# One product for the Q table and one for the spectrum, by an eighth turn in both angle tables of an S4 convolution and bilinear GLU kernel

## The chip, the cores and the metric

The kernel runs on one core of one Trainium2 chip. The metric is device time in microseconds, the median of several executions. A profiled execution, of its own time, supplies the traces.

## The reference

One block with adaptive layer norm, in float32, for L = 2048 tokens of width D = 640: first an S4 convolution with N = 192 complex states a channel, then a bilinear GLU of width F = 1536.

```python
dt = jnp.exp(log_dt)[:, None]
logdA = dt * (A_re + 1j * A_im);  dB = dt * (B_re + 1j * B_im)
P = jnp.exp(logdA[:, :, None] * l[None, None, :])          # D x N x L
K = jnp.einsum("dn,dnl,dn->dl", Cc, P, dB).real            # the kernel, D x L
...                                                        # y = irfft(rfft(u) * rfft(K)) + u * Dskip
h = layernorm(x) * (1 + ca) + sa;  x = x + ga * S4(h)
h = layernorm(x) * (1 + cb) + sb;  x = x + gb * (((h @ w_gate) * (h @ w_up)) @ w_down)
```

The six modulation rows sa, ca, ga, sb, cb, gb come from silu(c) @ w_mod.

## The kernel before, in words

The work falls into two parts. The first, up to about 525 us, makes the convolution kernel K, its spectrum and the spectrum of the normed input, multiplies the two and transforms back. The second is the GLU in split float32r products, on PE almost alone.

**Kernel generation.** There are 40 blocks n (`NK`), each of 16 channels of D, and ten halves hf of four blocks each. A power exp(logdA l) is split into a product of two factors P and Q, one for the coarse and one for the fine part of l, each with a magnitude (`EP`, `EQ`) and an angle. Angles are 32-bit integers in which 2^32 is a whole turn, so that adding them wraps by itself. Tables grow on POOL:

- `tab_ph` (L680, once a half, for the first half in two pieces a = 0 and 1) writes the low angles `LH`: column 0 is a copy (L698), column 1 an add (L699), and `double` (L678) makes columns 2 to 7. One half of the rows of LH is for P, the other for Q with the phase of the amplitude in it. L697 completes the high angles `DH`.
- `tab_eq` (L702) does the same for the magnitudes `LQ` (L708, L709, L678).
- `mk_ph`, `mk_eq` and `mk_ep` (all at L714 in `outer`) spread low and high parts into the block's tables `Ph`, `EQ` and `EP`, on POOL, for the next block.

ACT then makes a sine and a cosine of each angle (`trig`, L753, ACT instructions at L230) into a pair of PSUM banks `tr`, bank 0 the cosine and bank 1 the sine. The absolute value first and a quarter turn in the second call make the cosine. DVE multiplies by the magnitudes: `PtA` and `PtB` (L776, L796) for P, and `qmul` (L767) for Q. `QtA` covers 16 rows and `QtB` 8. Each Q row has 64 places. The first 32 (L769) hold the products with the angles in reversed order. The other 32 hold cosine times magnitude (L770) and minus sine times magnitude (L771). PE multiplies P and Q over the states: `kg_ma` (L811) from the A tiles, `kg_mb` (L826) from the B tiles, 32 small matmuls each, with the cosine half (c = 0) and the sine half (c = 1) added in PSUM, which gives the real part.

**Transforms.** `u_k` (L848) and `u_pre` (L872) do the first stage for K and for the input, `u_g` and `u_c` the second (`stage2`, L893). `u_c` (L919) multiplies the two spectra: real and imaginary part of K's spectrum (`kr`, `ki`, in PSUM) by both parts of H, in four products (L934 to L937) and two sums (L939, L940); then PE transforms back (L950), and `u_d` (L971, L978) ends it. Of the 20 products, 16 take all 128 channels at once and the last four are cut into two of 64 channels.

**Order.** Every engine works through its own queue in the order in which the program issues, which is written out by hand: a loop of 3 x 40 + 24 slots takes kg_aq, kg_ap and kg_b of block n in turn, issues the products of DVE in `MUL`, then POOL's tables for block n + 1, then PE's products, and fits all other jobs in by due times from the table `SCHED`. The buffers that two stages share (`Ph`, `PtA`, `TV`, `tr`) are two deep, and `QtA`, `QtB` and `PtB` one deep.

Of the kernel before, what the change touches and what calls it, by code (L numbers as in the profile page):

```python
# [12 lines left out]
I32 = mybir.dt.int32  # L13
AF = mybir.ActivationFunctionType
OP = mybir.AluOpType
# [3 lines left out]
P = 128  # L19
# [76 lines left out]
    d=(  # L96
# [5 lines left out]
    ),  # L102
# [68 lines left out]
    tr="abababababababababababababababababababababababababababababababababababababababababababababababababababababababababababab"  # L171
# [53 lines left out]
def tile_kernel(ctx: ExitStack, tc: tile.TileContext, I, out):  # L225
    nc = tc.nc
    V, S, G, PE, SY = nc.vector, nc.scalar, nc.gpsimd, nc.tensor, nc.sync

    def act(o, i, f=AF.Copy, **kw):
        return S.activation(o, i, f, **kw)  # L230

    const = ctx.enter_context(tc.tile_pool(name="const", bufs=1))
# [14 lines left out]
    shl = const.tile([P, 11], I32, name="shl")  # L247
    for k in range(11):
        V.memset(shl[:, k : k + 1], k + 1)
    mv1 = const.tile([P, 16, 2], F32, name="mv1")  # L250
    rs1 = const.tile([P, 16], F32, name="rs1")
    nm1 = const.tile([P, 16], F32, name="nm1")
# [8 lines left out]
    def ring(pool, shape, name, dtype=F32):  # L261

        return pool.tile(shape, dtype, name=name + next(slot[name]), bufs=1)
# [3 lines left out]
    def mark(*k):  # L267
        done[k] = done.get(k, 0) + 1

    def need(n, *k):  # L270

        assert done.get(k, 0) >= n, k
# [401 lines left out]
    def double(lo, powers, op):  # L674

        for w, p_ in zip((2, 4), powers):
            b = p_.unsqueeze(len(p_.shape)).to_broadcast(list(p_.shape) + [w])
            G.tensor_tensor(lo[..., w : 2 * w], lo[..., 0:w], b, op=op)  # L678

    def tab_ph(hf, a=None):  # L680

        need(1, "step", hf)
        if a != 1:
            need(1, "seeds", hf // 2)
        if hf:
            need(1, "ph", 4 * hf - 1)
        if a != 1:
            mark("lh", hf)
        dl, dh = DL[hf % 2], DH[hf % 3]
        sel = (lambda t: t) if a is None else (lambda t: t.rearrange("p (s a r) -> p s a r", a=2, r=24)[:, :, a])  # L690
        lh = LH if a is None else LH.rearrange("p (s a r) l -> p s a r l", a=2, r=24)[:, :, a]
        d = [sel(dl[:, k]) for k in range(4)]
        one = lambda t: t.unsqueeze(len(t.shape))
        if a != 1:
            for f in PSI.pop(hf):
                f()
        G.tensor_tensor(sel(dh[:, 3]), sel(dh[:, 1]), sel(dh[:, 2]), op=OP.add)  # L697
        G.tensor_copy(lh[..., 0:1], one(d[0]))  # L698
        G.tensor_tensor(lh[..., 1:2], one(d[0]), one(d[1]), op=OP.add)  # L699
        double(lh, d[2:], OP.add)  # L700

    def tab_eq(hf):  # L702
# [64 lines left out]
    def qmul(Qt, tr, e, R):  # L767

        return [lambda: V.tensor_tensor(Qt[:, :, :, 0:32], tr[:, :, :, ::-1], e[:, :, 0:32].unsqueeze(1).to_broadcast([P, 2, R, 32]), op=OP.mult),  # L769
                lambda: V.tensor_tensor(Qt[:, 0, :, 32:64], tr[:, 0], e[:, :, 32:64], op=OP.mult),  # L770
                lambda: V.scalar_tensor_tensor(Qt[:, 1, :, 32:64], tr[:, 1], -1.0, e[:, :, 32:64], op0=OP.mult, op1=OP.mult)]  # L771

    def kg_ap(n):
        PtA = OUT[n]["PA"]
# [3 lines left out]
    def kg_aq(n):  # L778
        QtA = pk.tile([P, 2, 16, 64], F32, name="QtA", bufs=1)
        OUT[n] = dict(QA=QtA, PA=ring(pk, [P, 2, 16, 32], "PtA"))  # L780
        ab = None
        if n:
            ab = OUT[n]["PA"].rearrange("p c r m -> p c (r m)")
            act(ab, PH[n].rearrange("p (a r) m -> p a (r m)", a=2)[:, :, 0:512], AF.Abs, scale=TURN)
            ab = ab[:, 1]
        tr = trig(PH[n].rearrange("p r m -> p (r m)")[:, 768:1280], ab)
        MUL.append(qmul(QtA, tr.rearrange("p c (r m) -> p c r m", m=32), EQ[n % 2][:, 0:16], 16))

    def kg_b(n):
        PtB = pk.tile([P, 2, 8, 32], F32, name="PtB", bufs=1)  # L790
        QtB = pk.tile([P, 2, 8, 64], F32, name="QtB", bufs=1)
        OUT[n].update(PB=PtB, QB=QtB)
        ep_ = EP[n % 2]
        tr = trig(PH[n].rearrange("p (a r) m -> p a (r m)", a=2)[:, :, 512:768])
        trv = tr.rearrange("p c (a r m) -> p c a r m", a=2, m=32)
        MUL.append([lambda: V.tensor_tensor(PtB, trv[:, :, 0], ep_[:, 16:24, :].unsqueeze(1).to_broadcast([P, 2, 8, 32]), op=OP.mult)]  # L796
                   + qmul(QtB, trv[:, :, 1], EQ[n % 2][:, 16:24], 8))
# [88 lines left out]
    def stage2(src, k0, r):  # L886

        need(1, "tw")
        for i in range(4):
            for c in range(2):  # L890
                for par in range(2):
                    k = 2 * i + par
                    PE.matmul(r[c][par * 64 : par * 64 + 64, i, :], t_tw[:, k0 + k, c, :], src[:, k, :], start=True, stop=True, tile_position=(0, par * 64))  # L893
        return r

    def banks():
        return [ring(PF[-1], [P, 4, P], "psf") for _ in range(2)]
# [21 lines left out]
    def u_c(db, qd, parts=1):  # L919

        k0, dn = 8 * qd, P // parts
        for d0 in range(0, P, dn):
            need(dn // 16, "F", db, d0)
            if parts == 1:
                r = banks()
            else:
                ps = ring(PF[-1], [P, 2, 4, dn], "psf")
                r = [ps[:, 0], ps[:, 1]]
            kr, ki = stage2(FS[db][:, k0 : k0 + 8, d0 : d0 + dn], k0, r)
            yield  # L930
            need(1, "GH", db, qd)
            H = GH[db, qd][..., d0 : d0 + dn]
            T = ring(fp, [P, 2, 4, dn], "TV")
            V.tensor_tensor(T[:, 0], kr, H[:, 0], op=OP.mult)  # L934
            V.tensor_tensor(T[:, 1], kr, H[:, 1], op=OP.mult)
            V.tensor_tensor(kr, ki, H[:, 1], op=OP.mult)
            V.tensor_tensor(ki, ki, H[:, 0], op=OP.mult)  # L937
            x = T if parts == 1 else H
            V.tensor_tensor(x[:, 0], T[:, 0], kr, op=OP.subtract)  # L939
            V.tensor_tensor(x[:, 1], T[:, 1], ki, op=OP.add)  # L940
            yield
        if parts > 1:
            x = GH[db, qd]
        need(1, "ti")
        r = banks()
        for i in range(4):
            for c in range(2):
                for par in range(2):
                    lo = par * 64
                    PE.matmul(r[par][:, i], t_ti[lo : lo + 64, qd * 4 + i, c, :], x[lo : lo + 64, c, i, :], start=c == 0, stop=c == 1, tile_position=(lo, 0))  # L950
        yield
        W = ring(fp, [P, 4, 2, P], "W")
        for par in range(2):
            act(W[:, :, par], r[par])
        WQ[len(PF) - 1].dma_start(WD[db][:, k0 : k0 + 8], W.rearrange("p i r d -> p (i r) d"))
        mark("WD", db)
# [329 lines left out]
    for db in range(NB):  # L1286
        if db:
            at(T0["q"][db - 1], u_seeds, db)
        for q in range(4):
            at(T0["pre"][db][q], u_pre, db, q)  # L1290
            at(T0["g"][db][q], u_g, db, q)
            at(T0["c"][db][q], u_c, db, q, 1 if db < NB - 1 else 2)
            at(T0["d"][db][q], u_d, db, q)
    for n in range(NK):
        at(T0["k"][n], u_k, n)
    for i, f in enumerate((tab_ph, tab_eq)):
        for hf in range(1, 2 * NB):
            at(T0["low"][i][hf - 1 : hf], once(f), hf)
# [17 lines left out]
    for i, _ in enumerate(gp0):  # L1316
        due(i - 100)
        if i == P_PH:
            tab_ph(0, 1)
            mk_ph(0, 1)  # L1320
        elif i == P_EP:
            mk_ep(0)
        elif i == P_MOD:
            mod_i()
    tab_eq(0)
    tab_ph(0, 0)
    mk_ph(0, 0)
    mk_eq(0)
# [538 lines left out]
```

## Time and profile before

| | us |
|---|---|
| median of 3 runs | 987.37 |
| lowest and highest | 986.79, 993.78 |
| the profiled execution, own time | 988.54 |
| its span, first to last instruction | 986.8 |
| busy in the span: PE, DVE, ACT, POOL | 889.2, 723.8, 579.4, 509.1 |
| mean granted clock of PE | 0.961 of full |

A row of the timeline has start, duration, engine, line, operation, what it writes and reads, and the shape; brackets give how long the engine stood idle before it and what ended that. A row of the chain has start, length, engine and line. A row of the stretches has the busy time of each engine in it with the number of instructions, then the granted clock (1.00 is full), the DMA share and GB/s. A row of the waits has the waiting engine and line, what it waited for, the sum in us, how often, and the longest.

### The profile page before, as it was taken

How to read it: one execution, taken by the hardware profiler on the slowest of the kernel's cores; microseconds unless marked ns; L12 is line 12 of the kernel's file. 1: busy time of each engine (PE TensorE's matmuls, PEld its weight loads, DVE VectorE, ACT ScalarE, POOL GpSimd, SP SyncE). 2: the span in 40 equal slices, each digit the busy share in tenths (PEclk: the TensorE clock that was granted, in tenths of full speed). 3: DMA queues.
4: the chain of work that ended last, by engine and by line, in shares of the span. 5: the costliest groups of instructions: out<-in, count | busy, mean ns of one | idle time of the engine just before them, and what ended most of it. 6: DMA issues, size and time to landing. Idle time of an engine off the chain costs nothing.

```text
span 986.8 us, 26765 instructions
## 1 busy us (share of the span) xinstructions
PE 889.2 (90%) x11134; PEld 720.2 (73%) x11134; DVE 723.8 (73%) x1400; ACT 579.4 (59%) x1076; POOL 509.1 (52%) x400
## 2 busy tenths in 40 slices
PE   4867898799789789988879999999999999999998
PEld 3565556586476557667736888889999788888998
DVE  8789568888978888794857665457676756578952
ACT  4869989987888887863336333334355443435430
POOL 5978899699879979960030354440113122222110
PEclk9877979999989889999999999999999999999999
DMA  7746654556246534658595665733564676658875
GB/s 254 262 142 223 204 194 147 172 165 185 77 153 181 152 105 126 205 172 257 189 273 191 222 191 182 242 125 113 184 217 124 197 231 222 222 179 292 237 244 187
DMA packets 158817, 188.54 MB, mean 191 GB/s; under 512 B 9828, under 2 KB 128360, under 8 KB 157544
## 3 DMA queue, kind: packets, MB, share of 16 engines
q1 hardware_dynamic: 149480, 155.51, 49.4%
q0 software_dynamic: 4752, 21.63, 7.6%
q10 hardware_dynamic: 4464, 9.70, 2.6%
q8 instruction: 87, 1.43, 0.6%
q14 instruction: 34, 0.28, 0.1%
HBM read 124.22 MB, written 62.59 MB: 189 GB/s over the span
## 4 chain that ended last, share of the span: by engine, by line
PE 55%; DVE 14%; ACT 12%; issue 10%; POOL 4%; DMA 3%; SPq 0%; DVEq 0%; POOLq 0%; ACTq 0%
PE pa L1078 18%; PE psg L1078 9%; PE pa L1502 9%; PE psfc L893 2%; PE kg L826 2%; PE kg L811 2%; PE psfa L893 2%; PE psfb L893 2%; ACT trb L230 1%; ACT tra L230 1%; PE psfc L950 1%; POOL EQ L714 1%; PE psfb L950 1%; PE pa L1554 1%; ACT L230 1%
## 5 line engine op out<-in xcount | busy, mean ns | idle before, releaser
L1055 POOL TENSOR_TENSOR tf<-wur,wgb 128x256 f32<-128x256 f32 x23 | 17.8, 775 | 246.9 <-DVE wtl L1026 199.5
L714 POOL TENSOR_TENSOR EQ<-LQ,RH 128x1536 f32<-128x1536 f32 x40 | 124.1, 3104 | 9.7 <-DVE QtB L771 9.5
L1026 DVE TENSOR_TENSOR wtl<-tf,wth 128x256 fp32r<-128x256 f32 (+1 forms) x72 | 36.7, 513 | 59.7 <-ACT wth L230 59.7
L714 POOL TENSOR_TENSOR Phb<-LH,DH 128x1536 int32<-128x1536 int32 x20 | 62.2, 3112 | 13.9 <-ACT tra L230 13.9
L714 POOL TENSOR_TENSOR EP<-LP,RH 128x768 f32<-128x768 f32 x40 | 66.0, 1650 | 0.0
L714 POOL TENSOR_TENSOR Pha<-LH,DH 128x1536 int32<-128x1536 int32 (+1 forms) x21 | 62.4, 2971 | 2.3 <-ACT trb L230 2.0
L1502 PE MATMUL pa<-wsg,sh 128*128 128x384 f32 (+1 forms) x304 | 58.4, 311 | 0.0
L826 PE MATMUL kg<-QtB,PtB 64*32 64x64 f32 x2560 | 48.7, 229 | 5.8 <-DVE QtB L770 5.3
L826 PEld LDWEIGHTS kg<-QtB,PtB 64*32 64x32 f32 x2560 | 41.7, 114 | 16.1 <-issue 7.2
L1502 PEld LDWEIGHTS pa<-wsg,sh 128*128 128x128 f32 x304 | 45.7, 189 | 0.0
L1541 POOL DMA_DIRECT2D wsg<-wdc x21 | 11.2, 531 | 66.5 <-PE pa L1554 35.6
L1026 DVE TENSOR_TENSOR wsg<-wga,wsg 128x640 fp32r<-128x640 f32 x36 | 33.7, 943 | 13.8 <-ACT wsg L230 13.8
L230 ACT ACTIVATE sh<-a 128x512 fp32r<-128x512 f32 x55 | 33.3, 625 | 13.9 <-PE psg L1554 6.2
L230 ACT ACTIVATE wsg<-wga 128x640 fp32r<-128x640 f32 x36 | 26.1, 730 | 25.0 <-PE pa L1502 12.8
L1026 DVE TENSOR_TENSOR sl<-a,sh 128x512 fp32r<-128x512 f32 x55 | 37.5, 702 | 4.0 <-ACT sh L230 4.0
L1078 PE MATMUL pa<-hh,wsg 128*128 128x512 f32 x150 | 40.2, 394 | 0.0
L1148 POOL TENSOR_SCALAR hfa<-xb,hr,hr 128x128 f32<-128x128 f32 x4 | 2.3, 577 | 67.5 <-DVE hr L283 67.5
L230 ACT ACTIVATE s<-pa 128x512 f32<-128x512 f32 x12 | 7.2, 598 | 48.5 <-PE pa L1078 48.5
L769 DVE TENSOR_TENSOR QtA<-tra,EQ 128x1024 f32<-128x1024 f32 x20 | 24.4, 1220 | 15.0 <-PE kg L811 7.0
L230 ACT ACTIVATE wth<-tf 128x256 fp32r<-128x256 f32 (+1 forms) x72 | 32.5, 481 | 4.9 <-DVE tf L1056 1.8
L230 ACT ACTIVATE a<-pa 128x512 f32<-128x512 f32 x12 | 7.2, 598 | 47.7 <-PE pa L1078 47.7
L1502 PE MATMUL pa<-wsg,sl 128*128 128x384 f32 (+1 forms) x152 | 34.4, 308 | 0.0
(656 smaller groups left out, 3125.6 us busy)
## 6 DMA issues: line engine op xcount, KB each, us to landing
wsg<-wdc POOLq DMA_DIRECT2D x21, 640.0 KB, 5.3
wgb<-B_w_gate SPq DMA_DIRECT2D x24, 320.0 KB, 4.6
wur<-B_w_up SPq DMA_DIRECT2D x24, 320.0 KB, 5.8
wsd<-wsg SPq DMA_DIRECT2D x12, 640.0 KB, 3.9
wga<-wdg SPq DMA_DIRECT2D x12, 640.0 KB, 3.9
wsg<-wsd POOLq DMA_DIRECT2D x12, 640.0 KB, 4.9
wdc<-xb SPq DMA_DIRECT2D x21, 320.0 KB, 3.3
TVb<-WD SPq DMA_DIRECT2D x22, 256.0 KB, 3.5
```

The costliest lines, as they stand in the source:

```text
L230: return S.activation(o, i, f, **kw)
L714: G.tensor_tensor(o.rearrange("p x (h l) -> p x h l", l=8), lo.unsqueeze(2).to_broadcast([P, rows, nh, 8]), hi.rearrange("p h x -> p x h") ...
L769: return [lambda: V.tensor_tensor(Qt[:, :, :, 0:32], tr[:, :, :, ::-1], e[:, :, 0:32].unsqueeze(1).to_broadcast([P, 2, R, 32]), op=OP.mult ...
L811: PE.matmul(kg[j * 32 : j * 32 + 32, dd, :], PtA[:, c, dl * 4 + j, :], QtA[:, c, dl * 4 + j, :], start=dd == 0 and c == 0, stop=False, til ...
L826: PE.matmul(kg[j * 32 : j * 32 + 32, dd, :], PtB[lo : lo + 64, c, r, :], QtB[lo : lo + 64, c, r, :], start=False, stop=dd == 7 and c == 1, ...
L893: PE.matmul(r[c][par * 64 : par * 64 + 64, i, :], t_tw[:, k0 + k, c, :], src[:, k, :], start=True, stop=True, tile_position=(0, par * 64))
L950: PE.matmul(r[par][:, i], t_ti[lo : lo + 64, qd * 4 + i, c, :], x[lo : lo + 64, c, i, :], start=c == 0, stop=c == 1, tile_position=(lo, 0))
L1026: V.tensor_tensor(lo, v, hi, op=OP.subtract)
L1055: E.tensor_tensor(t[:, 0:2], u[:, 0:2], g[:, 0:2], op=OP.subtract)
L1078: PE.matmul(ps, w[a][:, k], x[b][:, l], start=first and n == 0 and m == 0, stop=n == 2 and m == len(ks) - 1, skip_group_check=True)
L1502: PE.matmul(AC[tb][t][c], x[:, ts], w[:, cs], start=st, stop=f == NF - 1 and n == 2 and (c == 0 or t % 2 == 1))
L1541: G.dma_start(WD[q], wdc[:, q // 3, q % 3])
```

## The change

Both angle tables get an eighth of a turn (2^29) more: the low angles' column 0 becomes an add of a constant column `eighth` where it was a copy, and column 1 is built on column 0. With P and Q both turned by an eighth, cos(P')sin(Q') + sin(P')cos(Q') = sin(P' + Q') = cos(P + Q), so the second 32 places of Q take the sine and the cosine swapped, with no sign change, in one product over both. The difference of the two angles, in the first 32 places, is the same as before. Apart from that, `u_c` multiplies kr by both parts of H in one instruction, kr being read twice.

```diff
+    eighth = const.tile([P, 1], I32, name="eighth")
+    V.memset(eighth, 1 << 29)
...
-        G.tensor_copy(lh[..., 0:1], one(d[0]))
-        G.tensor_tensor(lh[..., 1:2], one(d[0]), one(d[1]), op=OP.add)
+        G.tensor_tensor(lh[..., 0:1], one(d[0]), one(eighth.to_broadcast([P, 192]) if a is None else eighth.unsqueeze(2).to_broadcast([P, 4, 24])), op=OP.add)
+        G.tensor_tensor(lh[..., 1:2], lh[..., 0:1], one(d[1]), op=OP.add)
         double(lh, d[2:], OP.add)
...
         return [lambda: V.tensor_tensor(Qt[:, :, :, 0:32], tr[:, :, :, ::-1], e[:, :, 0:32].unsqueeze(1).to_broadcast([P, 2, R, 32]), op=OP.mult),
-                lambda: V.tensor_tensor(Qt[:, 0, :, 32:64], tr[:, 0], e[:, :, 32:64], op=OP.mult),
-                lambda: V.scalar_tensor_tensor(Qt[:, 1, :, 32:64], tr[:, 1], -1.0, e[:, :, 32:64], op0=OP.mult, op1=OP.mult)]
+                lambda: V.tensor_tensor(Qt[:, :, :, 32:64], tr[:, ::-1], e[:, :, 32:64].unsqueeze(1).to_broadcast([P, 2, R, 32]), op=OP.mult)]
...
-            V.tensor_tensor(T[:, 0], kr, H[:, 0], op=OP.mult)
-            V.tensor_tensor(T[:, 1], kr, H[:, 1], op=OP.mult)
+            V.tensor_tensor(T, kr.unsqueeze(1).to_broadcast([P, 2, 4, dn]), H, op=OP.mult)
             V.tensor_tensor(kr, ki, H[:, 1], op=OP.mult)
             V.tensor_tensor(ki, ki, H[:, 0], op=OP.mult)
```

Each instruction changed is named after the line at which it stands before.

## The prediction

> **What bounds the kernel now.** I read the page first (busy shares, then the chain that ended last), then the engines by stage, then the chain in stretches of 20 us.
>
> ```profile
> PE 889.2 (90%) x11134; PEld 720.2 (73%) x11134; DVE 723.8 (73%) x1400; ACT 579.4 (59%) x1076; POOL 509.1 (52%) x400
> ...
> PE 55%; DVE 14%; ACT 12%; issue 10%; POOL 4%; DMA 3%; SPq 0%; DVEq 0%; POOLq 0%; ACTq 0%
> ```
>
> ```profile
> 20.00:440.00 420.00, 356.55 (x7709) 263.41 (x7707) 353.22 (x633) 346.65 (x634) 375.62 (x229) 0.91 0.54 170
> 440.00:525.00 85.00, 69.49 (x999) 49.38 (x995) 53.55 (x145) 31.03 (x56) 9.36 (x15) 0.98 0.77 231
> 525.00:986.00 461.00, 457.33 (x2406) 403.25 (x2406) 300.09 (x545) 189.68 (x363) 115.58 (x138) 1.00 0.62 202
> ```
>
> The second fence gives, for each stretch, the busy time of PE, PEld, DVE, ACT and POOL, then the granted clock and the DMA. From 525 us on PE is busy 457 of 461 us: that part is bound by PE and holds none of the edited lines. All edits lie before about 485 us. There, from 20 to 440 us, no engine is the bound alone: PE 85%, DVE 84%, ACT 83%, POOL 89%. The chain moves from engine to engine, so a microsecond taken from one engine counts only at the places where the chain stands on that engine. What is saved there passes on to the end whole, since the part after it runs its PE work at a fixed length.
>
> **DVE: 80 product pairs and 24 spectrum pairs become single instructions.** The cost of an instruction in a row is the step from its start to the next start, not its duration, because neighbours overlap:
>
> ```profile
> 436.10 0.68 DVE L769 TENSOR_TENSOR QtB<-trb,EQ 128x512 f32<-128x512 f32 x1
> 436.70 0.41 DVE L770 TENSOR_TENSOR QtB<-trb,EQ 128x256 f32<-128x256 f32 x1
> 437.03 0.41 DVE L771 SCALAR_TENSOR_TENSOR QtB<-trb,EQ 128x256 f32<-128x256 f32 x1
> 437.36 1.22 DVE L769 TENSOR_TENSOR QtA<-tra,EQ 128x1024 f32<-128x1024 f32 x1
> 438.49 0.68 DVE L770 TENSOR_TENSOR QtA<-tra,EQ 128x512 f32<-128x512 f32 x1
> 439.09 0.68 DVE L771 SCALAR_TENSOR_TENSOR QtA<-tra,EQ 128x512 f32<-128x512 f32 x1
> 439.69 0.68 DVE L934 TENSOR_TENSOR TVa<-psfa,ghc 128x512 f32<-128x512 f32 x1
> 440.29 0.68 DVE L935 TENSOR_TENSOR TVa<-psfa,ghc 128x512 f32<-128x512 f32 x1
> 441.07 0.70 DVE L936 TENSOR_TENSOR psfa<-psfb,ghc 128x512 f32<-128x512 f32 x1
> ```
>
> QtA (40 times): L770 and L771 take steps of 0.60 + 0.60 = 1.20 us. The new instruction has the shape of L769 on QtA, whose step is 438.49 - 437.36 = 1.13. Saved: 0.07. QtB (40 times): 0.33 + 0.33 = 0.66 against L769 on QtB, 436.70 - 436.10 = 0.60. Saved: 0.06. Spectrum (16 full and 8 half-wide pairs): from the start of L934 to the start of L936 are 1.38 us, of which the last 0.10 is the wait of L936, which overwrites what L935 reads. The new one: 1.22 + 0.10 = 1.32, saved 0.06; I take the same for the half-wide pairs. On DVE in all 40 x 0.07 + 40 x 0.06 + 24 x 0.06 = 6.6 us.
>
> That the swapped operand is read from the second PSUM bank backwards to the first is in no row. Its nearest is L769, which reads the same banks with the inner axis reversed at the same pace, so I take no cost. That L771's scaling by -1 goes is worth nothing: L770 and L771 last the same. Two bounds: 0 saved, if the new pattern costs as much as it spares, and 0.14 a pair (0.68 + 0.68 - 1.22), if the overlap of neighbours is lost on none of the rest.
>
> The Trainium skill (VectorE: DVE Perf Modes, "The DRAIN you can't avoid") says that the next VectorE operation does not start until the pipe is empty, and gives a float32 tensor_tensor as (N+151)/0.96 ns. By that alone a merged pair would save 157 ns, and 104 pairs 16.4 us, an estimate from that page. The trace does not bear it out: L771 starts 0.60 us after an L770 that lasts 0.68, which fits the same section's remark that an operation that is not held starts earlier.
>
> How much of the 6.6 us lies on the path:
>
> ```profile
> 172.97 0.61 DVE TVa L935
> ...
> 258.50 0.61 DVE QtA L771
> ...
> 439.17 0.60 DVE QtA L771
> ...
> 481.77 0.34 DVE TVa L935
> ```
>
> These are the first and last pieces of their kind in the chain. It holds 15 spectrum pairs (L934 with L935, 172.38 to 481.77 us) and 8 whole product pairs (L770 with L771, 257.90 to 439.17); in 5 more product pairs it touches one of the two only. So 23 x 0.065 = 1.5 us, at most 28 x 0.065 = 1.8. The other 5 us are hidden by waits of DVE for ACT and PE.
>
> One thing is late: PE's first four matmuls of a block need only the cosine half, which L770 alone gave, and now wait for the whole instruction.
>
> ```profile
> PE kg L826 <- DVE QtB L770: 5.3, 2, 3.9
> ```
>
> PE waited so twice, and the next four matmuls needed L771 anyway. I count it at nothing; the bound is the time of four small matmuls at those two places.
>
> **POOL: a copy becomes an add, and the next add must wait for it.**
>
> ```profile
> 191.93 0.59 POOL L697 TENSOR_TENSOR DH<-DH 128x192 int32<-128x192 int32 x1
> 192.47 0.55 POOL L698 COPY LH<-DL 128x192 int32<-128x192 int32 x1
> 192.87 0.61 POOL L699 TENSOR_TENSOR LH<-DL 128x192 int32<-128x192 int32 x1
> 193.56 0.94 POOL L678 TENSOR_TENSOR LH<-LH,DL 128x384 int32<-128x384 int32 x1
> ```
>
> L699 starts 0.40 us after the copy, before the copy has ended, since it reads only DL. In the changed kernel it reads column 0 of LH, which L698 writes. So L698 takes the step that L699 takes now ahead of L678, its reader: 0.69 us. That is 0.29 more, 11 times (nine whole, two half-wide that I price the same): 3.2 us on POOL. The broadcast column and the strided read of LH I price as nothing, since L678 and the big tables read both kinds now.
>
> ```profile
> L709 POOL TENSOR_TENSOR LQ<-RL 128x96 f32<-128x96 f32 x10 | 3.9, 393 | 0.0
> ...
> L708 POOL COPY LQ<-RL 128x96 f32<-128x96 f32 x10 | 3.6, 359 | 0.0
> ```
>
> The two rows are the nearest price of an add against a copy of one size: 34 ns. The Trainium skill (GPSIMD Engine Reference, "4.1 Engine selection") speaks against the change: there a two-input operation on GpSimd is about twice as slow as on VectorE, a one-input one about as fast. If the add cost twice its copy here, POOL would lose some 0.55 us more each time, 6 us in all; the two rows show a tenth instead.
>
> Is POOL's delay on the path? Once surely, near the start, where the chain runs through it:
>
> ```profile
> 21.25 0.30 POOL LH L698
> 21.55 0.27 POOL LH L699
> ```
>
> That is +0.29. Later, the big tables are made about one block ahead; where they come in just in time, the row shows what follows:
>
> ```profile
> 201.59 3.11 POOL L714 TENSOR_TENSOR EQ<-LQ,RH 128x1536 f32<-128x1536 f32 x1
> ```
>
> ```profile
> 204.73 1.23 DVE L769 TENSOR_TENSOR QtA<-trb,EQ 128x1024 f32<-128x1024 f32 x1 [0.52 <-POOL EQ L714]
> ```
>
> ```profile
> 209.60 0.69 DVE L796 TENSOR_TENSOR PtB<-trb,EP 128x512 f32<-128x512 f32 x1 [1.32 <-ACT trb L230]
> ```
>
> EQ ends at 204.70 and QtA starts at 204.73: no slack. But DVE idles 1.32 us for ACT soon after, so 0.29 is taken in there. And POOL itself stands still between its runs:
>
> ```profile
> POOL Phb L714 <- ACT tra L230: 13.9, 4, 6.4
> ...
> POOL EQ L714 <- DVE QtB L771: 9.5, 3, 6.0
> ```
>
> Both waits let a lag of 0.3 to 0.6 us vanish. If that cover were gone, all 3.2 us would count.
>
> The constant adds one memset at the head of DVE, ahead of a wait of 0.76 us for a load, and costs nothing:
>
> ```profile
> 3.62 0.17 DVE L320 TENSOR_SCALAR ex<-ldt 128x5 f32<-128x5 f32 x1 [0.76 <-DMA ldt<-A_log_dt]
> ```
>
> **Sum.** -1.5 on DVE (0 to -1.8), +0.3 on POOL (0.3 to 3.2): -1.2. Where the chain gets shorter by 0.06 at a time, the next path is often no longer than that behind, so I take -1.0, between -1.5 and 0. The profiled execution took 988.54 us (span 986.8), 1.2 above the median of 987.37; it would come to 987.5. Against the median: **986.4 us**, own range 985.8 to 987.4.
>
> **Rivals**, each from the median.
>
> *POOL becomes the bound.* For it: 375.62 of 420 us busy, and no slack at 204.73. Against it: its waits of 13.9 and 9.5 us, and 4% of the chain. Its place is the phase table ahead of each big table; it decides as soon as 0.29 us a time is not caught up by the next wait. Price 3.2 us with no gain left: 990.6, slower. By the Trainium skill's factor of two ("4.1 Engine selection") it would be 6 us more, 996.6.
>
> *DVE was the bound after all.* All 6.6 us arrive: 980.8. Against it: DVE idles 67 of the 420 us, and 14% of the chain is DVE.
>
> *The whole fixed part of an instruction is saved*, 0.14 x 104 = 14.6 us, and all of it on the path: 972.8. The steps above speak against it. It is what the Trainium skill's rule on the DRAIN would make of the change.
>
> *PE gets a lower clock.* The stretches differ:
>
> ```profile
> 20.00:181.00 161.00, 129.83 (x2311) 93.03 (x2309) 127.38 (x260) 135.91 (x249) 141.38 (x88) 0.85 0.60 200
> 181.00:259.00 78.00, 71.39 (x1636) 49.85 (x1638) 67.66 (x117) 61.27 (x110) 75.53 (x46) 1.00 0.54 165
> ```
>
> PE is 92% busy where the clock is full and 81% where it is 0.85. Suppose moved gaps cost the clock from 181 to 440 us too. The chain's PE share there is at most the kernel's 55%, 142 of 259 us, less what already runs slow (the mean from 20 to 440 is 0.91); I take 80. At 0.85 they last 80 x (1/0.85 - 1) = 14 us longer: 1001.4. It decides, by more than 1%, from about 0.89 on. Against it: shorter DVE steps close gaps rather than open them.
>
> *The swapped read is slow and eats the saving*: 0 from DVE, +0.3 from POOL: 987.7.
>
> **How the numbers follow.** Forecast 0.62, POOL 0.14, DVE 0.08, whole fixed part 0.05, clock 0.07, slow read 0.04. One per cent, 9.9 us, is about what a measurement of this kernel can tell from no change. Faster by more: only the whole fixed part, 0.05. Slower by more: only the clock, 0.07. Within: 0.88. The range takes in the POOL and DVE cases: 980.5 to 991.2; left out are 0.12 and a little of their tails.
>
> **What would show it.** Right: 1217 to 1225 ns for the new product on QtA, about 681 on QtB, some 6 us less between first and last DVE start only where DVE was already in a row; L698 near 0.6 us with L699 starting 0.69 after it; the stretch after 525 us unchanged in length; the stage before it about 1 us shorter. Wrong: a new product well over 1225 ns; DVE waiting for EQ again and again as at 204.73 (then POOL rules); a granted clock from 20 to 440 us off 0.91 by more than 0.03, or a first GLU matmul earlier by 5 us or more.

## The result, and the profile after

| | before | changed |
|---|---|---|
| median of 22 runs, us | 987.14 | 983.68 |
| lowest and highest | 983.7, 993.78 | 980.63, 987.31 |
| the profiled execution, own time and span | 988.54, 986.8 | 987.31, 985.5 |

The changed kernel takes 0.9959 of the time of before (95% interval 0.9944 to 0.9975): 4.0 us less, between 2.5 and 5.5. (The ratio is that of the means; the medians differ by 3.5 us.) The forecast was 1.0 us. Its profiled execution happens to be the slowest of the 22, so the two traces are compared by instruction and by stage, not by their ends.

Busy shares and chain, from the page of the changed kernel:

```profile
PE 892.4 (91%) x11134; PEld 725.6 (74%) x11134; DVE 717.3 (73%) x1297; ACT 579.4 (59%) x1076; POOL 513.1 (52%) x400
...
PE 56%; ACT 14%; DVE 13%; issue 10%; POOL 4%; DMA 3%; SPq 0%; POOLq 0%; ACTq 0%; DVEq 0%
```

DVE has 103 instructions fewer (104 merged away, one memset more) and 6.5 us less busy time; POOL has 4 us more. The stretches of the changed kernel (busy PE, PEld, DVE, ACT, POOL, then the clock):

```profile
20.00:440.00 420.00, 360.50 (x7676) 268.00 (x7677) 346.90 (x537) 345.99 (x633) 377.99 (x229) 0.90 0.53 169
```

```profile
525.00:985.00 460.00, 454.53 (x2410) 402.09 (x2408) 298.65 (x545) 190.57 (x365) 116.87 (x138) 1.00 0.63 203
```

DVE's new steps, from the timeline:

```profile
437.88 0.68 DVE L771 TENSOR_TENSOR QtB<-trb,EQ 128x512 f32<-128x512 f32 x1
438.47 0.68 DVE L772 TENSOR_TENSOR QtB<-trb,EQ 128x512 f32<-128x512 f32 x1
439.07 1.22 DVE L771 TENSOR_TENSOR QtA<-tra,EQ 128x1024 f32<-128x1024 f32 x1
440.20 1.22 DVE L772 TENSOR_TENSOR QtA<-tra,EQ 128x1024 f32<-128x1024 f32 x1
441.33 1.22 DVE L935 TENSOR_TENSOR TVa<-psfa,ghc 128x1024 f32<-128x1024 f32 x1
442.65 0.70 DVE L936 TENSOR_TENSOR psfa<-psfb,ghc 128x512 f32<-128x512 f32 x1
```

The merged product (now L772) steps 1.13 us on QtA and 0.60 on QtB, the merged spectrum product (L935) 1.32 to the next: the three prices of the forecast. The swapped read costs nothing.

POOL's new steps:

```profile
190.14 0.59 POOL L699 TENSOR_TENSOR DH<-DH 128x192 int32<-128x192 int32 x1
190.69 0.55 POOL L700 TENSOR_TENSOR LH<-DL,eighth 128x192 int32<-128x192 int32 x1
191.31 0.70 POOL L701 TENSOR_TENSOR LH<-LH,DL 128x192 int32<-128x192 int32 x1
192.09 2.60 POOL L680 TENSOR_TENSOR LH<-LH,DL 128x384 int32<-128x384 int32 x2
```

The add that took the copy's place lasts as long as the copy (0.55 us), but the next add waits for it. From the first low-angle instruction to `double` it is 192.09 - 190.69 = 1.40 us against 1.09 before.

The surprise stands where nothing was edited. The first GLU product, before and changed:

```profile
525.37 1.17 PE L1078 MATMUL pa<-hh,wsg 128*128 128x512 f32 x4
```

```profile
526.44 1.17 PE L1078 MATMUL pa<-hh,wsg 128*128 128x512 f32 x4
```

From there to the end of the span it is 461.4 us before and 459.1 changed, although PE's instructions are the same and the clock is full in both. Groups of matmuls in that stage (sum in us, mean in ns), before and then changed:

```profile
L1502 PE MATMUL pa<-wsg,sh 128*128 128x384 f32 x152 | 48.8, 342 | 0.0
L1078 PE MATMUL psg<-sh,wsuh 128*128 128x512 f32 x51 | 14.5, 393 | 0.0
```

```profile
L1502 PE MATMUL pa<-wsg,sh 128*128 128x384 f32 x152 | 47.6, 334 | 0.0
L1078 PE MATMUL psg<-sh,wsuh 128*128 128x512 f32 x51 | 14.4, 390 | 0.0
```

The single matmul is 8 ns shorter in the one form and 3 in the other, in a stage that PE fills. The ends of matmuls are modelled in a trace, so their steps are the firmer reading: from start to start, the 152 of the first form take 27.4 us before and 26.1 changed.

### The profile page after: what moved, and what is told of

Same layout as the page of the kernel before. It is cut to its first block, busy times and chain, and to the rows that moved or that the text cites. A ratio compares the mean times of both kernels' runs of the same rounds, so it can differ in the third digit from the quotient of the medians.

```text
span 985.5 us, 26662 instructions
## 1 busy us (share of the span) xinstructions
PE 892.4 (91%) x11134; PEld 725.6 (74%) x11134; DVE 717.3 (73%) x1297; ACT 579.4 (59%) x1076; POOL 513.1 (52%) x400
## 4 chain that ended last, share of the span: by engine, by line
PE 56%; ACT 14%; DVE 13%; issue 10%; POOL 4%; DMA 3%; SPq 0%; POOLq 0%; ACTq 0%; DVEq 0%
PE pa L1078 18%; PE psg L1078 9%; PE pa L1502 7%; PE kg L812 2%; PE kg L827 2%; PE psfc L894 2%; PE psfb L894 2%; PE psfc L950 2%; ACT trb L230 2%; ACT L230 2%; PE psfa L894 1%; ACT tra L230 1%; DVE QtA L772 1%; DVE QtA L771 1%; PE psfc L873 1%
## 5 line engine op out<-in xcount | busy, mean ns | idle before, releaser
L230 ACT ACTIVATE wsg<-wga 128x640 fp32r<-128x640 f32 x36 | 26.1, 730 | 24.8 <-PE pa L1502 12.1
L1078 PE MATMUL pa<-sh,wth 128*128 128x512 f32 x110 | 34.0, 390 | 0.4 <-ACT a L230 0.4
```

Of the source, the lines that this page charges most:

```text
L1078: PE.matmul(ps, w[a][:, k], x[b][:, l], start=first and n == 0 and m == 0, stop=n == 2 and m == len(ks) - 1, skip_group_check=True)
```

## The experiments

Theory A is the forecast's: the edited instructions on the chain count, nothing else. B: DVE's steps count by half or more. C: the clock. After the first four runs theory L joined them: the new constant moves the addresses of other tiles, and the GLU's matmuls depend on these. The ratios are to executions of the kernel before that ran alongside; there were 12 of each kernel, 22 of the changed one, six of pool_more and one of right_part. The column "GLU" below is the time from the first GLU product to the end of the span in the one profiled execution. It hardly varies, unlike the part before it, whose end lies between 520 and 528 us in the kernels that differ by little.

| kernel | GLU, us | ratio to before (95%) |
|---|---|---|
| before; again, as aa_before | 461.4; 461.7 | 1.0011 (0.9988 to 1.0035) |
| changed | 459.1 | 0.9959 (0.9944 to 0.9975) |
| products_only | 458.6 | 0.9963 (0.9945 to 0.9981) |
| spectrum_only | 462.0 | 0.9987 (0.9965 to 1.0008) |
| tables_only | 458.9 | 0.9980 (0.9962 to 0.9999) |
| pad_32 | 459.0 | 0.9970 (0.9957 to 0.9984) |
| no_shift | 461.4 | 0.9986 (0.9969 to 1.0003) |
| pad_64 | 461.3 | 0.9990 (0.9973 to 1.0007) |
| right_32 | 459.1 | 0.9966 (0.9947 to 0.9985) |
| right_part | 464.1 | one run, 988.44 us |
| dve_more | 461.4 | 1.0018 (0.9994 to 1.0042) |
| pool_more | 458.7 | 1.0081 (1.0056 to 1.0106) |
| seeds_right | 458.9 | 0.9966 (0.9943 to 0.9988) |

**aa_before.** The kernel before, unedited.

> The kernel before, unchanged, against itself. Theory A (only the edited instructions that lie on the chain of the one profiled execution count: 23 to 28 pairs x 0.065 us, less 0.3 us on POOL) and theory B (DVE's steps count for about half of their whole sum of 6.6 us, because the chain runs elsewhere in other executions) expect a ratio of 1.000 within 0.0015 and a mean granted clock of 0.960, as in the changed kernel's executions (0.955 to 0.970). Theory C (the gain is a clock that the changed kernel is granted, not the shorter steps) expects a mean clock here lower by 0.004 or more.

The mean clock of its executions was 0.959, that of the changed kernel's 0.960. The difference that C needs is not there.

**products_only.** The change without its last hunk.

> The angle tables and the merged Q product alone; the spectrum's two products stay apart. DVE is spared 80 x 0.065 = 5.2 us, POOL is burdened by about 3 us. Theory A: 8 to 13 pairs on the chain, -0.5 to -0.85, and +0.3 on POOL: ratio 0.9995 to 0.9998 (-0.2 to -0.5 us). Theory B: half of 5.2 = -2.6 us, ratio 0.9974. Theory C: no change in time at an equal clock.

0.9963, near the whole change. That looked like B, until the next two.

**spectrum_only.** The last hunk alone.

> The spectrum's merged product alone; angles and Q products as before. DVE is spared 24 x 0.06 = 1.4 us, POOL nothing. Theory A: 15 of the 24 pairs are on the chain: -0.9 us, ratio 0.9991. Theory B: half of 1.4, -0.7 us. A gain of 2 us or more would speak against both: then the merged product would do more than its step says.

0.9987, with an interval that takes in what A expects (0.9991) and what B does (0.9993): these cannot be told apart here.

**tables_only.** No DVE step is saved, POOL has the longer tables of the change. Against the kernel before, `qmul` differs so:

```diff
-                lambda: V.tensor_tensor(Qt[:, 0, :, 32:64], tr[:, 0], e[:, :, 32:64], op=OP.mult),
-                lambda: V.scalar_tensor_tensor(Qt[:, 1, :, 32:64], tr[:, 1], -1.0, e[:, :, 32:64], op0=OP.mult, op1=OP.mult)]
+                lambda: V.tensor_tensor(Qt[:, 0, :, 32:64], tr[:, 1], e[:, :, 32:64], op=OP.mult),
+                lambda: V.tensor_tensor(Qt[:, 1, :, 32:64], tr[:, 0], e[:, :, 32:64], op=OP.mult)]
```

> The eighth of a turn in the tables with the swapped operand, but in two products (neither of them scaled by -1), and the spectrum as before: DVE's steps are those of before, POOL has the longer add. Theories A and B: +0.3 us, ratio 1.0003, at most 1.001; if POOL is the bound: +3 us, ratio 1.003. If the swapped read itself were faster or slower than the two products of before, DVE's rows would show it.

0.9980, a little faster (0.9962 to 0.9999), where A and B alike expected no gain. A kernel that saves no step on DVE and adds work on POOL came out 2 us ahead, and its GLU was as short as that of the changed kernel. The GLU was short in just the kernels that hold the constant `eighth`. In the program's allocation this [128, 1] tile takes 32 bytes, and every tile placed after it on that side moves up by 32: `wsg` from 57920 to 57952, `hh1` from 23104 to 23136. The tiles of the right side (`sh` at 132576, `wth` at 176096) stay.

**pad_32.** The shift alone, with nothing else changed:

```diff
+    pad = const.tile([P, 1], I32, name="pad")
+    V.memset(pad, 0)
     mv1 = const.tile([P, 16, 2], F32, name="mv1")
```

> The kernel before with one unused [128, 1] constant where the changed kernel has its eighth: every tile allocated after it on the left side (the GLU's weights and activations too) lies 32 bytes further; no instruction differs but one memset. So far the three kernels that hold the constant ran from the first GLU product to the end in 458.6 to 459.1 us, the three that do not in 461.4 to 462.0. Theory L (the addresses do it): 459 us again here, ratio 0.997 (-2.9 us). Theory P (the longer POOL add shifts something, or the missing scale by -1): 461.7, ratio 1.000.

```profile
L1504 PE MATMUL pa<-wsg,sh 128*128 128x384 f32 x152 | 47.7, 334 | 0.0
```

0.9970 and 459.0 us, as theory L expects. An unused constant brings 3.0 us (1.6 to 4.2), and the GLU alone is shorter by 2.4.

**no_shift.** The whole change, with the tiles where they were:

```diff
-    shl = const.tile([P, 11], I32, name="shl")
+    shl = const.tile([P, 12], I32, name="shl")
+    eighth = shl[:, 11:12]
+    V.memset(eighth, 1 << 29)
...
-    eighth = const.tile([P, 1], I32, name="eighth")
-    V.memset(eighth, 1 << 29)
```

> The changed kernel with the eighth as a twelfth column of an existing constant, whose padded place it does not outgrow: every tile lies where it lay before. All instructions are those of the changed kernel. Theory L: from the first GLU product to the end 461.7 us, as before, and in all only the forecast's own sum, -1.2 us (ratio 0.9988, 0.998 to 1.000). Theory B (DVE's steps count by half or more): -3.5 us, ratio 0.9964, as in the changed kernel.

```profile
520.18 1.17 PE L1078 MATMUL pa<-hh,wsg 128*128 128x512 f32 x4
```

```profile
L1502 PE MATMUL pa<-wsg,sh 128*128 128x384 f32 x152 | 49.0, 343 | 0.0
L1078 PE MATMUL psg<-sh,wsuh 128*128 128x512 f32 x51 | 14.5, 393 | 0.0
```

The span of this execution is 981.6, so the GLU takes 461.4 us, with the matmuls of before. In all 0.9986: -1.4 us (-3.1 to +0.3), where A's sum is -1.2. B's 0.9964 lies outside the interval. This is the measurement of the edited instructions by themselves; it does not tell A's sum from no gain at all.

**pad_64.** As pad_32, with `const.tile([P, 16], I32)`.

> The kernel before with an unused constant of 64 bytes: the left tiles lie 64 bytes further. If the offset within 64 bytes is what counts: 461.7 us for the GLU, ratio 1.000. If any other place is better than that of before, or the offset within 128 bytes counts: 459, ratio 0.997.

```profile
L1504 PE MATMUL pa<-wsg,sh 128*128 128x384 f32 x152 | 48.6, 341 | 0.0
```

The GLU takes 461.3 us, as before. So not every shift helps: 32 bytes do, 64 do not.

**right_32.** The left side stays, the right side's GLU tiles move down by 32 bytes:

```diff
+    gpad = gp.tile([P, 1], F32, name="gpad", bufs=1)
+    V.memset(gpad, 0.0)
     ps_a = ctx.enter_context(tc.tile_pool(name="ps_a", bufs=1, space=PSUM))
```

> The kernel before with an unused constant at the end of the right side's GLU tiles, which moves these (sums, activations and the split up weights) 32 bytes down; the left side (gate and down weights, first activations) stays. Before, the left tiles start at multiples of 64 bytes and the right ones 32 past one; the changed kernel has both 32 past one. If it counts that both sides share their offset: 459 us for the GLU, ratio 0.997. If the left side's own offset counts: 461.7, ratio 1.000.

```profile
L1504 PE MATMUL pa<-wsg,sh 128*128 128x384 f32 x152 | 47.6, 334 | 0.0
L1078 PE MATMUL psg<-sh,wsuh 128*128 128x512 f32 x51 | 14.4, 390 | 0.0
```

0.9966, 459.1 us. Now both sides start at multiples of 64; in the changed kernel both start 32 past one; before, they differ. What counts is the offset between the two sides, not either of them.

**right_part.** As right_32, with the pad in the middle: the activations `sh`, `sl`, `hh2`, `hl2` move, with some sums of DVE, and the up weights `wth`, `wsuh` do not.

> The kernel before with the unused constant in the middle of the right side: sums a10 to a14, z, s6 and the split activations hh2, hl2, sh, sl lie 32 bytes lower, the up weights (wth, wtl, wsuh, wsul, tf) and the products a0 to a4 and a15 to a23 stay. If the activations that PE reads as one operand matter, the matmuls of the down product (pa<-wsg,sh, 384 wide) last 334 ns instead of 342 and the GLU 459 us; if the products that are read and written by DVE and ACT meanwhile matter, 342 ns and 461.7 us. A split outcome (one form of matmul faster, another not) would say that each has its own partner.

```profile
L1078 PE MATMUL pa<-sh,wth 128*128 128x512 f32 x110 | 34.7, 396 | 0.3 <-ACT a L230 0.3
...
L1502 PE MATMUL pa<-wsg,sh 128*128 128x384 f32 x152 | 47.7, 334 | 0.0
...
L1078 PE MATMUL psg<-sh,wsuh 128*128 128x512 f32 x51 | 14.6, 394 | 0.0
...
L1554 PE MATMUL pa<-wsg,sh 128*128 128x320 f32 x136 | 33.2, 310 | 0.0
```

The split outcome. Where the two operands of a matmul now share their offset (`wsg` with `sh`), it takes 334 ns instead of 342. Where they have become different (`sh` with `wth`), it takes 396 instead of 391:

```profile
L1078 PE MATMUL pa<-sh,wth 128*128 128x512 f32 x110 | 34.0, 391 | 0.4 <-ACT a L230 0.4
```

That is the row of before. The GLU is 464.1 us in this one run, worse than any other.

**dve_more.** On the kernel before, the first Q product in two, so 80 DVE steps more:

```diff
-        return [lambda: V.tensor_tensor(Qt[:, :, :, 0:32], tr[:, :, :, ::-1], e[:, :, 0:32].unsqueeze(1).to_broadcast([P, 2, R, 32]), op=OP.mult),
+        return [lambda: V.tensor_tensor(Qt[:, 0, :, 0:32], tr[:, 0, :, ::-1], e[:, :, 0:32], op=OP.mult),
+                lambda: V.tensor_tensor(Qt[:, 1, :, 0:32], tr[:, 1, :, ::-1], e[:, :, 0:32], op=OP.mult),
```

> The kernel before with the first Q product (angles reversed) in two instructions instead of one, by cosine and sine half: DVE has 80 steps more of 0.06 to 0.07 us, 5.2 us in all, and no tile moves. Theory A (a quarter of such steps lies on the chain, 23 to 28 of 104): +1.2 to 1.4 us, ratio 1.0013. Theory B (half or more): +2.6 us or more, ratio 1.0026 to 1.005.

+1.8 us (-0.6 to +4.1) for 5.2 us of steps: the middle is a third. Inconclusive between a quarter and a half; the whole is outside.

**pool_more.** The changed kernel with 22 further adds on POOL:

```diff
+        for _ in range(2):
+            G.tensor_tensor(lh[..., 1:2], lh[..., 0:1], one(d[1]), op=OP.add)
         double(lh, d[2:], OP.add)
```

> The changed kernel with column 1 of the low angles computed three times instead of once: POOL has 22 adds more of 0.69 us, 15 us in all, 1.4 us ahead of every half's tables. If POOL's waits cover its lag, as forecast, the time is that of the changed kernel plus the 1.4 us at the start that lie on the chain and little else: ratio to the kernel before 0.997 to 0.999. If POOL is the bound: 15 us more, ratio 1.011. In between, the ratio tells how much of a lag of 1.4 us a half the waits take in.

1.0081 against 0.9959 of the changed kernel: 12 us, give or take 3. The trace shows 15.8 put in: an added add takes a step of 0.76 us, not the 0.69 expected. Of DVE's waits before the GLU, the one that sums up to most is now for POOL:

```profile
DVE QtA L773 <- POOL EQ L718: 13.7, 8, 3.8
```

In the changed kernel the same wait is short:

```profile
DVE QtA L771 <- POOL EQ L716: 1.6, 2, 1.2
```

So POOL's cover is thin: tables_only shows no sign that the 0.3 us a half of the change get through, and most of 1.4 us more do. The mean clock was lower here as well, 0.954 against the changed kernel's 0.960; what part of the 12 us goes with that was not taken apart.

**seeds_right.** The eighth on DVE, where it converts the seeds; POOL as before; the right side moved:

```diff
-            V.tensor_copy(g5(Dl[h])[:, 0, :, 1, :], ps[:, 1, hs[h]])
+            V.tensor_scalar(g5(Dl[h])[:, 0, :, 1, :], ps[:, 1, hs[h]], float(1 << 29), None, op0=OP.add)
...
-            V.tensor_scalar(psi, ps[:, 1], 4294967296.0 / math.pi, None, op0=OP.mult)
+            V.tensor_scalar(psi, ps[:, 1], 4294967296.0 / math.pi, float(1 << 30), op0=OP.mult, op1=OP.add)
```

> A version meant to beat both. The merged products as in the changed kernel, but the eighth is added on DVE, where it converts the seeds of the angles (a scalar add in a conversion that is there anyway, and a quarter turn in the phase's scaling), so POOL's instructions are those of before; and the right side's GLU tiles lie 32 bytes lower. Sum: -1.5 us on DVE, nothing on POOL, -2.9 us in the GLU: -4.4 us, ratio 0.9955, some 0.3 us under the changed kernel. If POOL's add costs more than forecast, it gains more than that over the changed kernel.

0.9966: faster than before, and not to be told from the changed kernel (0.9959). The 0.3 us that POOL's add was forecast to cost is below what these runs resolve; this version does not beat the changed kernel.

## Why the prediction was right or wrong

*Direction and range: right, in good part by luck.* Faster, within 1%; 983.7 us lies in the range 980.5 to 991.2, but below the forecast's own range of 985.8 to 987.4. Most of the gain came from a shift of addresses that the forecast did not have. In the one run of right_part, a shift of other tiles by the same 32 bytes made the GLU 2.5 us longer.

*DVE's steps: right.* 1.13, 0.60 and 1.32 us are the steps forecast. The Trainium skill's rule (VectorE: DVE Perf Modes, "The DRAIN you can't avoid"), read as 157 ns spared for each merged pair, is not borne out here: 0.06 to 0.07 us are, since the pairs had overlapped already. PE's longer wait for the whole product, which I counted at nothing, went from 5.3 to 7.1 us, twice in each trace; whether that is the edit's doing is not shown.

*POOL's price: right in sum, wrong in its parts.* 0.31 us a time against 0.29. The wait costs 0.22 of it: the first instruction's step goes from 0.40 to 0.62, not to 0.69. The other 0.09 is the next add's step, from 0.69 to 0.78, which I had priced at nothing; its new input, the strided column of LH, is the likely reason, but was not tried apart. The Trainium skill (GPSIMD Engine Reference, "4.1 Engine selection") puts an operation with two inputs on GpSimd at about half the speed of VectorE. Read as the prediction did, as an add that takes twice its copy, this does not show: the add takes 0.55 us, the copy took 0.55.

*The share of the path: fits, but loosely.* no_shift measures the edits alone at -1.4 us (-3.1 to +0.3); the sum said -1.2 and I took -1.0. The interval excludes the 3.5 us of B, has half of DVE's steps (-3.3, or -3.0 with POOL's price) at its edge, and takes in no gain at all. Of the five pairs that I took to be touched in one product only, the chain touches both products of the one at 385.68 us. That POOL's waits cover its lag holds for the 0.3 us of this change as far as tables_only can tell: its -2.0 us, less the 2.7 of the GLU, leaves +0.7, with an interval from -1.1 to +2.6, where the whole lag would be 3.3. For a larger lag it does not hold.

*The step that failed* is the one that sounded safest: the part after 525 us would run "its PE work at a fixed length", and the constant "adds one memset ... and costs nothing". It moved 32 bytes of address under the GLU's tiles. That part's length changed by 2.7 us (mean of the seven profiled executions with both sides at one offset 458.9, of the six with the old offset 461.6), two thirds of the gain. Nothing speaks against the forecast's own sum for the edits; a term was missing. I had named "the stretch after 525 us unchanged in length" as a sign of being right: it was the sign that showed the fault. The other sign, a first stage shorter by 1 us, cannot be read in one execution: the first GLU product starts at 525.37 us before and at 526.44 changed, in traces where that time varies by 8 us.

*Rivals.* POOL as the bound did not come, but stands close. DVE as the bound and the whole fixed part would have shown in no_shift and did not. The clock was the same in the mean, 0.960 against 0.959. The slow read is refuted by DVE's rows.

## What to carry to other kernels

Instructions priced in steps, not durations, came out as forecast, and the share of them that lies on the chain agreed with the runs as far as these resolve 1 us, which is not far. But in a stage that one engine fills, look also at where the tiles lie: a new constant, however small, can shift every tile behind it, and before a gain is put down to an edit, the edit should be run without its shift and the shift without the edit. When a part of the trace that holds no edited line changes its length, that is where to look first.

## What the runs showed of the hardware that I had not expected

In this kernel the time of some float32r matmuls depends on the start addresses of SBUF tiles modulo 64 bytes. With the operands `wsg` and `sh` 32 bytes apart in that measure, the 384-wide one takes 341 to 343 ns in all six kernels with such tiles. At equal offsets it takes 334 in all eight, whether both lie at 0 (right_32) or both at 32 (changed). In right_part, `sh` against `wth` went from 391 ns at equal offsets to 396 at different ones. Over 461 us of PE work this is 2.7 us less with both sides at one offset, and 2.5 us more with right_part's mixture.

The rule does not cover every row. The 320-wide matmul of the same operands takes 309 or 310 ns throughout, the 256-wide one 279 or 280. And `sh` with `wsuh` fell from 393 to 390 ns in the changed kernel, where neither of them had moved against the other. There the traces point to neighbours in PE's order: of the 51 matmuls, the 33 with a `wsg` product among the four just before them fell from 394 to 390 ns on average, the other 18 from 390 to 389. So a pair at different offsets also slows some matmuls that follow it. How it does that, and what in the memory makes the difference, stays open.
